# TensorE's six steady steps as one loop, in a decode-attention and gated-MLP kernel

## The chip, the cores and the metric

The kernel runs on one core of a Trainium2 chip. The metric is the device time of one execution in microseconds (us). Before the change the median of three runs is 380.52 us (380.44 to 380.76).

## The reference, cut to what matters

One token x (1024 wide) goes through two branches, and a sigmoid gate g mixes them.

```python
q = (x @ wq)                      # 32 heads of 128, in 4 groups of 8 that share one K/V head
scores = q . k_cache * 128**-0.5  # k_cache, v_cache: 4 K/V heads x 65536 positions x 128, bf16
a = softmax(scores) . v_cache @ wo
z = gelu(x @ w_in); z1, z2 = halves(z); z2 = layernorm(z2)
b = (z1 * (w_sp * z2 + b_sp)) @ w_out
g = sigmoid(sum(x * gate_w))
out = g * a + (1 - g) * b         # 1 x 1024
```

Each of the two caches is 67 MB. Together with the weights the kernel reads 162 MB and computes little on each byte.

## The kernel before, in words

**Loads.** The large loads leave SyncE (SP) on one DMA queue in a fixed order, the list `stream`: wq, K pieces, w_in, w_out, then in turn a pair of K pieces and a pair of V pieces (8 MB each), and at the end wo in five loads. They land in a ring of five slots (`RING`). `issue()` (L378) records the next load as soon as every piece that owned its place has been read; `done(key)` marks a piece as read. `halves` (L336) says which half of a pair lies first. `few_rows` (L398) carries a part of the last rows of wq in eight small loads of 4 x 5 and 4 x 3 rows of 1 KB.

**Pieces.** A K/V head is cut in four pieces of 16384 positions. A K piece is worked off in four quarters (`k_piece`, L542): VectorE (DVE) turns one quarter into one of two buffers `kt` (L548), and TensorE (PE) makes eight matmuls with it into the PSUM tensor `scp` (recorded in the helper `mm`, L261 and L263). After two pieces `score_pair` (L565) copies the scores to SBUF and takes their maximum. ScalarE (ACT) makes the exponentials and their sums `lp` (`exp_pair`, L580), DVE turns them (`pt_pair`, L585), and PE multiplies with a V piece into `ob` (`pv_piece`, L590, 32 matmuls).

**Steps.** The loop at L799 runs six steady steps, each with two K pieces, two V pieces and one `exp_pair`. In every second step a head group is closed: the maximum of the next group (`max_first`, `max_second`, with one f32 matmul at L574 that spreads it), the sums (`out_first`, two f32 matmuls at L609), the reciprocal (`out_second`), the scaling of `ob` (`out_third`), four matmuls that turn the result into columns (L627 for groups 0 and 1, L631 for groups 2 and 3), and `out_fourth`, which writes `ovz`. Groups 0 and 1 share one half-wide form, groups 2 and 3 have another. After the six steps come the last four V pieces, wo in pieces, one DVE copy (L827) and the store.

**Order.** `Recorder` notes every operation with what it reads and writes. `plan` (L57) works out the semaphore waits that are needed, and `emit` (L96) writes each engine's program straight out, operation by operation. All engines run in the order of recording; PE's program has 2313 machine instructions.

Of the kernel before, what the change touches and what calls it, by code (L numbers as in the profile page):

```python
# [13 lines left out]
class Op:  # L14
    __slots__ = ("eng", "fn", "deps", "inc", "idx", "count", "dma", "vis")


class Recorder:
# [4 lines left out]
    def __init__(self):  # L23
        self.ops = []
        self.writer = {}
        self.readers = {}
        self.dma_count = {}
        self.ahead = 0
        self.early = 0

    def op(self, eng, fn, r=(), w=(), dma=None):
        o = Op()
        o.eng, o.fn, o.inc, o.count = eng, fn, False, 0
        o.dma = None
        deps = {}
        for k in r:
            if k in self.writer:
                deps[id(self.writer[k])] = (self.writer[k], True)
        for k in w:
            if k in self.writer:  # L40
                deps.setdefault(id(self.writer[k]), (self.writer[k], False))
            for x in self.readers.get(k, ()):
                deps.setdefault(id(x), (x, False))
        o.deps = list(deps.values())
        for k in r:
            self.readers.setdefault(k, []).append(o)
        for k in w:
            self.writer[k] = o
            self.readers[k] = []
        if dma is not None:  # L50
            self.dma_count[dma] = self.dma_count.get(dma, 0) + 16
            o.dma = (dma, self.dma_count[dma])
        o.idx = len(self.ops)
        self.ops.append(o)
        return o

    def plan(self):  # L57
        known = {e: {} for e in self.ENGINES}
        waits = []
        for o in self.ops:  # L60
            kn = known[o.eng]
            need = {}
            for d, raw in o.deps:
                if d.dma is None and d.eng == o.eng and (not raw or o.eng == "PE"):
                    continue
                key = ("dma", d.dma[0]) if d.dma else d.eng
                at = d.dma[1] if d.dma else d.idx
                if kn.get(key, -1) >= at:
                    continue
                if key not in need or need[key][0] < at:  # L70
                    need[key] = (at, d)
            for key, (at, d) in list(need.items()):
                for k2, (at2, d2) in need.items():
                    if k2 != key and d2.vis.get(key, -1) >= at:
                        need.pop(key)
                        break
            mine = []
            for key, (at, d) in need.items():
                d.inc = True
                mine.append(d)  # L80
                kn[key] = max(kn.get(key, -1), at)
                for k2, a2 in d.vis.items():
                    if kn.get(k2, -1) < a2:
                        kn[k2] = a2
            waits.append(mine)
            o.vis = dict(kn)
            if o.dma is None:
                o.vis[o.eng] = o.idx
        counts = {e: 0 for e in self.ENGINES}
        for o in self.ops:  # L90
            if o.inc and o.dma is None:
                counts[o.eng] += 1
                o.count = counts[o.eng]
        return waits

    def emit(self, nc):  # L96
# [5 lines left out]
        def run(eng, handle):  # L102
            for o, ws in zip(self.ops, waits):
                if o.eng != eng:
                    continue
                for d in ws:
                    if d.dma:
                        handle.wait_ge(dsem[d.dma[0]], d.dma[1])
                    else:
                        handle.wait_ge(sems[d.eng], d.count)  # L110
# [3 lines left out]
                elif o.inc:  # L114
                    last.then_inc(sems[eng], 1)
# [12 lines left out]
        run("PE", nc.tensor)  # L128
# [7 lines left out]
        run("DVE", nc.vector)  # L136


def bass_gated_mix__gqa_block_cached__mixer_gmlp__decode_kernel(
# [53 lines left out]
    for name, n in [  # L193
# [3 lines left out]
        ("XT", KC), ("WB", 2), ("WBB", 4), ("ONEB", 128),  # L197
        ("MAXC", 2 * total), ("LP", 2 * total), ("COLS", 2 * 64), ("DM", 64), ("ONES", 256), ("QALL", 128), ("OVZ", 32 * OC + 31), ("E4Z", 128), ("MHALF", 4),
# [17 lines left out]
    idb, bm, ones = ab("IDB", 128), af("BM", 128), af("ONES", 128)  # L216
    sel, m16, mq = ab("SEL", 512), af("M16", 16), af("MQ", 16)
    xT, wb, wbb, oneb = ab("XT", KC), ab("WB", 2), af("WBB", 2), ab("ONEB", 128)
    qpad, qall = ab("QPAD", 4 * QP), ab("QALL", 128)
    maxc, lp, colt = af("MAXC", total), af("LP", total), af("COLS", 64)  # L220
# [3 lines left out]
    dm = af("DM", 32)  # L224
    psb, psb2 = ab("PSB", 1024), ab("PSB", 2048)
    osc, ot = ab("PSB", 512), af("PSB", 128, 256)
# [51 lines left out]
    P("POOL", lambda e: e.memset(ones, 1.0), w=["ones"])  # L278
# [31 lines left out]
    def load(keys, src, off):  # L310

        n = len(stream)
        w = src.shape[1]
# [22 lines left out]
    def halves(kind, n):  # L336

        a, b = (kind, n), (kind, n + 1)
        return [b, a] if n % 4 == 2 and n > 2 else [a, b]
# [20 lines left out]
    load([("wo", 0, 0)], rows(A_wo, 0, 16), WO_AT[0])  # L360
# [17 lines left out]
    def issue():  # L378

        while issued[0] < len(stream):  # L380
            n = issued[0]
            keys, off, src = stream[n]
            w = src.shape[1]
# [8 lines left out]
            P("SP", lambda e, o=OFF["RING"] + off, w=w, src=src[:, :w]: e.dma_start(arena[:, o:o + w], src),  # L392
# [82 lines left out]
    P("PE", lambda e: e.matmul(mb[:, 0:2], oneb[0:1, :], wb[0:1, :], start=True, stop=True),  # L475
# [6 lines left out]
    P("PE", lambda e: e.matmul(tb[:, 0:1], ones[0:8, :], col(C_GS)[0:8, :], start=True, stop=True),  # L482
# [59 lines left out]
    def k_piece(n, p):  # L542
        if n % NP == 0 and p == 0:
# [4 lines left out]
        P("DVE", lambda e: e.transpose(ktb(i).bitcast(F32), sl[:, 4096 * p:4096 * (p + 1)].bitcast(F32)),  # L548
          r=keys[4 * p:4 * p + 4], w=[("kt", i % NKT)])
# [12 lines left out]
        P("PE", f, r=["qpad", ("kt", i % NKT)], w=[KSC(n)])  # L562

    def score_pair(j):
        P("DVE", lambda e: e.tensor_scalar(scs(j), scp[:, :], 0.0, None, op0=ALU.add, op1=ALU.max,  # L565
                                           accum_out=maxc[:, j:j + 1]),
          w=[("sc", j % 2), ("mx", j), KSC(0), KSC(1)])

    def max_first(g):
# [4 lines left out]
        P("PE", lambda e: e.matmul(mb[:, 0:32], bm, dm, start=True, stop=True), r=["bm", "dm"], w=["mb"])  # L574

    def max_second(g):
        P("DVE", lambda e: e.tensor_reduce(gcol(g, K_NB), mb[:, 0:32], AXX, ALU.min), w=[("nb", g), "mb"])  # L577

    def exp_pair(j):
        P("ACT", lambda e: e.activation(psb2, scs(j), ACTF.Exp, bias=gcol(j // 2, K_NB), scale=SCALE,  # L580
                                        accum_out=lp[:, j:j + 1]),
          r=[("sc", j % 2), ("nb", j // 2)], w=["psb", ("lp", j)])

    def pt_pair(j):
        P("DVE", lambda e: e.transpose(ptsb2, psb2), r=["psb"], w=[("ptsb", 0), ("ptsb", 1)])  # L585
# [4 lines left out]
    def pv_piece(n):  # L590
        u = n % NP
        sl, keys = use(("v", n))

        def f(e):
            for i in range(16):
                b, t, cg = i // 8, 2 * (i % 8), i % 2
                for h in range(2):
                    ins = mm(e, h > 0, ob[64 * cg:64 * (cg + 1), 512 * h:512 * (h + 1)],
                                   ptsb(n)[:, 512 * b + 32 * t:512 * b + 32 * t + 64],
                                   vw(sl, 128 * (16 * b + t + h), [[4096, 4], [1, 128]]), start=(u == 0 and i < 2),  # L600
                                   stop=(u == NP - 1 and i >= 14), tile_position=(0, 64 * cg), skip_group_check=True)
            return ins
        P("PE", f, r=[("ptsb", n % 2)] + keys, w=["ob"])
        done(("v", n))

    def out_first(g):
        def f(e):
            for h in range(2):
                ins = e.matmul(mb[:, 0:1], bm, lp[:, 2 * g + h:2 * g + h + 1], start=(h == 0), stop=(h == 1))  # L609
            return ins  # L610
        P("PE", f, r=["bm", ("lp", 2 * g), ("lp", 2 * g + 1)], w=["mb"])

    def out_second(g):
        P("DVE", lambda e: e.reciprocal(gcol(g, K_RL), mb[:, 0:1]), w=[("rl", g), "mb"])  # L614
# [3 lines left out]
    def out_third(g):  # L618
        P("DVE", lambda e: e.tensor_scalar(osc, ob[:, 0:512], gcol(g, K_FA), None, op0=ALU.mult),
          r=[("fh", g)], w=["psb", "ob"])  # L620
        P("DVE", lambda e: e.scalar_tensor_tensor(osc, ob[:, 512:1024], gcol(g, K_FB), osc, op0=ALU.mult, op1=ALU.add),  # L621
          r=[("fh", g), "psb"], w=["psb", "ob"])

        def f(e):
            for c in range(4):
                if g < 2:
                    ins = e.matmul(mb[64 * g:64 * (g + 1), 0:128], vw(sel, 128 * c, [[2, 64]]),  # L627
                                   osc[:, 128 * c:128 * (c + 1)], start=(c == 0), stop=(c == 3),
                                   tile_position=(0, 64 * g), skip_group_check=True)
                else:  # L630
                    ins = e.matmul(mb[:, 0:128], sel[:, 128 * c:128 * (c + 1)], osc[:, 128 * c:128 * (c + 1)],  # L631
                                   start=(c == 0), stop=(c == 3))
            return ins
        P("PE", f, r=["sel", "psb"], w=["mb"])

    def out_fourth(g):

        p0, n, a, m = (64 * g, 64, 8, bm) if g < 2 else (0, 128, 16, mq)
        b, z = 128 // a, 31 + (0 if g < 2 else 256 * g)
        P("DVE", lambda e: e.tensor_tensor(vw(ot, 0, [[b, a], [1, b]], p0, n), vw(mb, 0, [[b, a], [1, b]], p0, n),  # L640
                                           vw(m, 0, [[1, a], [0, b]], p0, n), ALU.mult), r=["mq", "bm"], w=["psb", "mb"])

        def red(e):
            with nc.allow_low_precision(reason="one term is not zero"):
                return e.tensor_reduce(vw(ovz, z, [[32, b]], p0, n), vw(ot, 0, [[1, b], [b, a]], p0, n), AXX, ALU.add)
        P("DVE", red, r=["psb"], w=[("ovec", g)])

# [130 lines left out]
    def gmax(g):  # L778
        max_first(g)
        max_second(g)  # L780

    def out_rest(g):
        out_second(g)
        out_third(g)
        out_fourth(g)

# [9 lines left out]
    gmax(0)  # L796
    exp_pair(0)
    pt_pair(0)
    for i in range(6):  # L799
        k_step(2 * i + 4)  # L800
        k_step(2 * i + 5)
        score_pair(i + 2)
        pv_piece(2 * i)
        if i % 2:
            gmax((i + 1) // 2)
        exp_pair(i + 1)
        pv_piece(2 * i + 1)
        if i % 2:
            out_first(i // 2)
        pt_pair(i + 1)  # L810
        if i % 2:
            out_rest(i // 2)
# [5 lines left out]
    out_first(3)  # L818
    wo_rows()
    out_rest(3)  # L820
# [40 lines left out]
```

## Time and profile before

| what | value |
|---|---|
| median of three runs | 380.52 us |
| profiled execution | 380.59 us |
| its span, from first to last instruction | 379.3 us |
| mean granted TensorE clock | 0.838 |
| busy: PE, DVE, ACT | 229.9, 205.6, 23.3 us |
| HBM read | 162.01 MB, 427 GB/s over the span |

The span is what the views divide up; about 1.3 us of the execution lie outside it. "Busy" is the time in which an engine has at least one instruction running; the chain of waits follows the work that ended last back to what released it. The DMA table has one row for each queue and kind: packets, megabytes, and the share of the time of 16 DMA engines that their packets took.

### The profile page before, as it was taken

The page shows a single profiled execution, that of the slowest core. Times are in us where ns is not written, and L with a number is a line of the kernel's source. Part 1 is how long each engine was busy: PE and PEld are TensorE (multiplying, and loading weights), DVE is VectorE, ACT ScalarE, POOL GpSimd, SP SyncE. Part 2 cuts the span into 40 slices and gives each one's busy share as a digit, 9 for nine tenths or more (in the row PEclk, how much of TensorE's full clock was granted, in tenths as well). Part 3 has the DMA queues.
Part 4 walks back from the last instruction along what each step waited for, and adds up shares of the span by engine and source line. Part 5 has one row for each costly group of instructions (what it writes and reads, how often), then busy time and mean ns, then how long its engine had stood idle before and what let it go on. Part 6 is the DMA issues. An engine that isn't in the chain of part 4 may idle for free.

```text
span 379.3 us, 2599 instructions
## 1 busy us (share of the span) xinstructions
PE 229.9 (61%) x1452; PEld 57.9 (15%) x844; DVE 205.6 (54%) x168; ACT 23.3 (6%) x24; POOL 9.3 (2%) x36
## 2 busy tenths in 40 slices
PE   0062289566648934895389328951995189737296
PEld 0011011011201200121012001220111011201024
DVE  1411487778479625965496249745873387412020
ACT  1000000010420000002200000022000000220000
POOL 1400000000000000000000000000000000000000
PEclk9997589798959985998599959995899589958599
DMA  9999999999999999999999999999999999999896
GB/s 436 435 415 408 433 419 422 442 456 438 408 435 442 435 444 422 422 442 435 442 437 442 429 422 429 444 442 435 429 408 430 442 435 442 437 442 435 384 432 273
DMA packets 3822, 162.17 MB, mean 428 GB/s; under 512 B 484, under 2 KB 612, under 8 KB 868
## 3 DMA queue, kind: packets, MB, share of 16 engines
q1 hardware_dynamic: 3776, 162.01, 98.9%
q8 instruction: 9, 0.15, 0.1%
q10 hardware_dynamic: 36, 0.00, 0.0%
q14 instruction: 1, 0.01, 0.0%
HBM read 162.01 MB, written 0.00 MB: 427 GB/s over the span
## 4 chain that ended last, share of the span: by engine, by line
DMA 61%; PE 17%; DVE 17%; SPq 2%; ACT 1%; issue 1%
DMA arena<-in_A_k_cache_dram 46%; DVE arena L548 16%; DMA arena<-in_A_wo_dram 8%; DMA arena<-in_A_v_cache_dram 7%; PE scp L261 7%; PE scp L263 6%; SPq L409 2%; PE obt L261 2%; PE obt L263 1%; DVE arena L585 1%; PE fbt L766 1%; ACT arena L580 1%; DVE arena L670 0%; DVE arena L668 0%; PE fbt L714 0%
## 5 line engine op out<-in xcount | busy, mean ns | idle before, releaser
L548 DVE STREAM_TRANSPOSE arena<-arena 128x2048 f32<-128x2048 f32 x64 | 143.0, 2284 | 54.9 <-DMA arena<-in_A_k_cache_dram 40.1
L261 PE MATMUL scp<-arena 128*128 128x512 bf16 (+1 forms) x274 | 111.6, 424 | 94.4 <-DVE arena L548 93.9
L263 PE MATMUL scp<-arena 128*128 128x512 bf16 (+1 forms) x275 | 110.2, 418 | 0.0
L261 PE MATMUL obt<-arena 128*64 128x512 bf16 (+2 forms) x334 | 60.7, 404 | 15.1 <-DMA arena<-in_A_v_cache_dram 14.9
L263 PE MATMUL obt<-arena 128*64 128x512 bf16 (+2 forms) x333 | 60.1, 400 | 0.0
L261 PEld LDWEIGHTS scp<-arena 128*128 128x128 bf16 (+1 forms) x274 | 27.5, 104 | 205.1 <-issue 103.9
L585 DVE STREAM_TRANSPOSE arena<-arena 128x2048 bf16<-128x2048 bf16 x7 | 16.2, 2311 | 27.0 <-PE obt L263 24.8
L580 ACT ACTIVATE arena<-arena 128x2048 bf16<-128x2048 f32 x8 | 16.0, 2002 | 217.2 <-DVE arena L577 194.1
L261 PEld LDWEIGHTS obt<-arena 128*64 128x64 bf16 (+1 forms) x334 | 17.7, 109 | 65.3 <-issue 58.5
L565 DVE TENSOR_SCALAR_CACHE_REDUCE arena<-scp 128x2048 f32<-128x2048 f32 x8 | 18.3, 2292 | 16.0 <-PE scp L263 16.0
L614 DVE RECIPROCAL arena<-mbt 128x1 f32<-128x1 f32 x4 | 0.6, 138 | 17.5 <-PE mbt L609 17.5
L588 DVE STREAM_TRANSPOSE arena<-arena 128x1024 bf16<-128x1024 bf16 x2 | 2.5, 1245 | 12.9 <-PE obt L263 12.9
L536 POOL COPY arena<-arena 32x32 bf16<-32x32 bf16 x16 | 3.3, 204 | 227.4 <-PE scp L263 207.7
L467 PE MATMUL scp<-arena 8*128 8x1 bf16 x8 | 0.7, 198 | 13.0 <-DVE arena L462 13.0
L627 PE MATMUL mbt<-arena 128*64 128x128 bf16 x8 | 1.3, 314 | 7.7 <-DVE arena L621 7.7
L766 PE MATMUL fbt<-arena 128*32 128x128 bf16 x128 | 4.2, 220 | 1.2 <-DMA arena<-in_A_wo_dram 1.2
L280 DVE MEMSET mbt<- 128x512 f32 x1 | 0.5, 485 | 7.7 <-PEq L846 7.7
L513 DVE CAST arena<-obt 97x1024 bf16<-97x1024 f32 x1 | 1.2, 1224 | 6.2 <-PE obt L507 6.2
L475 PE MATMUL mbt<-arena 1*128 1x2 bf16 x1 | 0.2, 158 | 7.2 <-DMA arena<-in_B_b_sp_dram 7.2
L827 DVE CAST arena<-fbt 36x128 bf16<-36x128 f32 x1 | 0.3, 283 | 7.3 <-PE fbt L766 7.3
L477 DVE COPY arena<-mbt 128x2 f32<-128x2 f32 x1 | 0.2, 158 | 7.3 <-PE mbt L475 7.3
L577 DVE TENSOR_REDUCE arena<-mbt 128x1 f32<-128x32 f32 x4 | 0.8, 192 | 6.0 <-PE mbt L574 6.0
(99 smaller groups left out, 62.5 us busy)
## 6 DMA issues: line engine op xcount, KB each, us to landing
arena<-in_A_k_cache_dram SPq DMA_DIRECT2D x2, 4096.0 KB, 31.7
arena<-in_A_wq_dram SPq DMA_DIRECT2D x1, 8064.0 KB, 21.7
arena<-in_B_w_in_dram SPq DMA_DIRECT2D x1, 7168.0 KB, 28.9
arena<-in_A_wo_dram SPq DMA_DIRECT2D x1, 4096.0 KB, 38.5
arena<-in_B_w_out_dram SPq DMA_DIRECT2D x1, 3584.0 KB, 20.2
arena<-in_A_wo_dram SPq DMA_DIRECT2D x1, 2048.0 KB, 27.6
arena<-in_A_wo_dram SPq DMA_DIRECT2D x1, 1280.0 KB, 30.3
arena<-in_A_wo_dram SPq DMA_DIRECT2D x1, 512.0 KB, 31.0
```

The source lines that it names most:

```text
L261: return e.matmul(*a, **kw)
L263: one = e.matmul(*a, **kw).ins
L409: P("SP", lambda e, a=a, b=b: e.dma_start(a, b), w=[("few", lo + j0)] + ([] if lo + j0 else [("slot", x) for x in gr]), dma="few%d" % (lo ...
L513: P("DVE", lambda e: e.tensor_copy(psb[0:97, :], ob[0:97, :]), w=["psb", "ob"])
L536: P("POOL", lambda e, pb=pb: e.tensor_copy(vw(qpad, 24 + 32 * pb, [[QP, 4], [1, 8]], 32 * pb, 32), vw(qall, 8 * g, [[32, 4], [1, 8]], 32 * ...
L548: P("DVE", lambda e: e.transpose(ktb(i).bitcast(F32), sl[:, 4096 * p:4096 * (p + 1)].bitcast(F32)), r=keys[4 * p:4 * p + 4], w=[("kt", i % ...
L565: P("DVE", lambda e: e.tensor_scalar(scs(j), scp[:, :], 0.0, None, op0=ALU.add, op1=ALU.max, accum_out=maxc[:, j:j + 1]), w=[("sc", j % 2) ...
L580: P("ACT", lambda e: e.activation(psb2, scs(j), ACTF.Exp, bias=gcol(j // 2, K_NB), scale=SCALE, accum_out=lp[:, j:j + 1]), r=[("sc", j % 2 ...
L585: P("DVE", lambda e: e.transpose(ptsb2, psb2), r=["psb"], w=[("ptsb", 0), ("ptsb", 1)])
L588: P("DVE", lambda e: e.transpose(ptsb(n), ab("PSB", 1024, 1024 * (n % 2))), r=["psb"], w=[("ptsb", n % 2)])
L627: ins = e.matmul(mb[64 * g:64 * (g + 1), 0:128], vw(sel, 128 * c, [[2, 64]]), osc[:, 128 * c:128 * (c + 1)], start=(c == 0), stop=(c == 3) ...
L766: ins = e.matmul(fb[32 * b:32 * (b + 1), 0:QW], ovz[:, z:z + 32], sl[:, o:o + QW], start=False, stop=(i == 3 and c == 7), tile_position=(0 ...
```

## The change

- PE's part of the six steps is emitted once and runs in a hardware loop of six turns. A wait in the loop reads its threshold from a register, which a register addition then raises. For this every turn must have the same instructions and equal steps of every counter: `even()` adds to some of DVE's increments. The waits inside are only those named by `on=`.
- Every step now has the spread matmul (one, of 34 columns instead of 32: maximum and sums together) and the four turning matmuls, also the steps that close no group. `out_first` and its two f32 matmuls go.
- DVE gets `sums` (a copy of 128x2 into `dm`), a `tensor_reduce` of 128x2 in `out_second`, and `clear` (a memset of `ob`, 128x1024) ahead of the loop and after each closed group. Matmuls into `ob` always add.
- All four head groups leave in the form that groups 2 and 3 had. wo's first load has rows in two blocks of 8 x 128 (256 packets of 16 KB instead of 128 of 32 KB). V pairs keep one order of halves. `osc` gets a place of its own.
- The wait for q's layout (`qpad`) moves from PE to the K transposition on DVE.

The diff, cut to its core:

```diff
+    def even(self):
+        body = [o for o in self.ops if o.loop]
+        told = {o.loop[1] for o in body if o.inc}
+        for o in body:
+            o.inc = o.loop[1] in told
...
                 for d in ws:
-                    if d.dma:
-                        handle.wait_ge(dsem[d.dma[0]], d.dma[1])
+                    sem, n = (dsem[d.dma[0]], d.dma[1]) if d.dma else (sems[d.eng], d.count)
+                    if o.loop:
+                        reg, step = count[d.dma[0] if d.dma else d.eng, o.loop[1]]
+                        handle.wait_ge(sem, reg)
+                        handle.reg_add(reg, reg, step)
                     else:
-                        handle.wait_ge(sems[d.eng], d.count)
+                        handle.wait_ge(sem, n)
...
+        lead = next(o.idx for o in self.ops if o.loop)
+        run("PE", nc.tensor, lambda o: not o.loop and o.idx < lead)
+        for reg, n in begin:
+            nc.tensor.reg_mov(reg, n)
+        with nc.Fori(0, turns, engines=[mybir.EngineType.PE]):
+            run("PE", nc.tensor, lambda o: o.loop and o.loop[0] == 0)
+        run("PE", nc.tensor, lambda o: not o.loop and o.idx > lead)
...
-    load([("wo", 0, 0)], rows(A_wo, 0, 16), WO_AT[0])
+    load([("wo", 0, 0)], A_wo[0:2048, :].rearrange("(g p c) n -> p g (c n)", g=2, p=128), WO_AT[0])
...
+    def sums():
+        return P("DVE", lambda e: e.tensor_copy(dm[:, 32:34], lp), r=[("lp", 0), ("lp", 1)], w=["dm"], mark="g")
+    def spread_columns(on=None):
+        P("PE", lambda e: e.matmul(mb[:, 0:34], bm, dm, start=True, stop=True), r=["bm", "dm"], w=["mb"], on=on and [on])
+    def clear():
+        P("DVE", lambda e: e.memset(ob, 0.0), w=["ob"])
...
     for i in range(6):
+        R.begin(i)
         k_step(2 * i + 4)
         k_step(2 * i + 5)
-        score_pair(i + 2)
+        known = score_pair(i + 2)
+        if i % 2:
+            max_first((i + 1) // 2)
+            known = sums()
         pv_piece(2 * i)
+        spread_columns(known)
         if i % 2:
-            gmax((i + 1) // 2)
+            max_second((i + 1) // 2)
+            out_second(i // 2)
         exp_pair(i + 1)
         pv_piece(2 * i + 1)
+        known = pt_pair(i + 1)
         if i % 2:
-            out_first(i // 2)
-        pt_pair(i + 1)
+            known = out_third(i // 2)
+        turn_heads(known)
         if i % 2:
-            out_rest(i // 2)
+            out_fourth(i // 2)
+            clear()
```

## The prediction, as put on record

> **What bounds the kernel now.** I read the page first: slices and DMA table, then the chain.
>
> ```profile
> DMA  9999999999999999999999999999999999999896
> ...
> q1 hardware_dynamic: 3776, 162.01, 98.9%
> q8 instruction: 9, 0.15, 0.1%
> ...
> DMA 61%; PE 17%; DVE 17%; SPq 2%; ACT 1%; issue 1%
> ```
>
> The data queue keeps the 16 DMA engines busy for 98.9% of the span, in every slice but the last. So the stream of 162 MB is the bound. PE (61% busy) and DVE (54%) stand in the chain only because a load is issued when they have freed its place. The chain in order of time shows the end:
>
> ```profile
> 345.07 30.26 DMA arena<-in_A_wo_dram
> 375.46 1.80 PE fbt L766 x56
> 377.27 0.42 PE fbt L766 x8
> 377.72 0.28 DVE arena L827
> ```
>
> The last load lands at 377.23, and 2.1 us of matmuls, copy and store follow. The time can change in three ways: the stream starves, the DMA engine that ends last gets more or less to do, or the tail changes.
>
> **How much cover there is.** The timeline of the first two steady steps:
>
> ```profile
> 135.93 0.33 SPq L392 DMA_DIRECT2D arena<-in_A_v_cache_dram  x1
> 136.02 2.31 DVE L585 STREAM_TRANSPOSE arena<-arena 128x2048 bf16<-128x2048 bf16 x1 [4.82 <-PE obt L263]
> 145.33 2.31 DVE L548 STREAM_TRANSPOSE arena<-arena 128x2048 f32<-128x2048 f32 x1 [7.00 <-DMA arena<-in_A_k_cache_dram]
> ```
>
> A step without a closing group ends its DVE work at 138.33 and idles 7.0 us until the next K pair lands. The next step closes a group and idles 3.92 us:
>
> ```profile
> 176.63 0.13 DVE L614 RECIPROCAL arena<-mbt 128x1 f32<-128x1 f32 x1
> ...
> 180.03 2.00 ACT L580 ACTIVATE arena<-arena 128x2048 bf16<-128x2048 f32 x1 [6.97 <-DVE arena L645]
> ...
> 183.92 2.31 DVE L548 STREAM_TRANSPOSE arena<-arena 128x2048 f32<-128x2048 f32 x1 [3.92 <-DMA arena<-in_A_k_cache_dram]
> ```
>
> The second cover is the issue. I set each issue of SP beside the first completion of the load ahead of it. The V issue at 135.93 is followed by a K landing at 143.32: 7.4 us ahead. In the loop the K issues are 5.8 us (118.15 against 123.98) to 7.2 us ahead, the V issues 7.4 to 8.3. The very first issue, at 0.00, had its first packet at 1.18. So the shortest cover is 5.83 - 1.18 = 4.6 us.
>
> **The change part by part.**
>
> *DVE.* `clear` writes 128x1024 f32 in PSUM: twice the 128x512 memset (485 ns), 0.97 us. `sums` is near the 128x2 copy of L477, 0.16 us. The 128x2 reduce lies between a 128x1 operation, 0.16, and the 128x32 reduce, 0.19. The wider `out_fourth` costs nothing: 0.29 + 0.39 us at 128 partitions against 0.28 + 0.36. Together about 1.3 us in each closing step. The reciprocal and scaling (0.4) move ahead of `pt_pair`, so about 0.9 us of it lies before the next K landing, where 3.92 us are idle: nothing on the path. The first `clear` must wait until ACT has copied `ob` (100.93); it delays the first maximum from 102.05 to about 102.3, and the K issue at 118.15 by as much, out of 4.6.
>
> *PE.* A plain step gains one f32 spread (0.41 us, L574) and four turning matmuls (0.40 to 0.63, L631 and L627): 1.0 us. A closing step loses the two f32 matmuls of L609 (0.61). In a plain step the turning matmuls wait for `pt_pair`, which ended at 138.33. Behind them in PE's queue stand the K matmuls, which can't start before 145.33 + 2.3: 9 us of cover. In a closing step they stand where they stood. The spread waits for `score_pair` (131.20 in the first step), which is done before the V piece ahead of it (about 132): no wait. V's issue comes 0.4 us later, out of at least 6.2.
>
> *Loop control.* No row shows a register wait, a register addition or a branch. Their bound from below is nothing, because PE waits for data between them. From above I take the 0.9 us of idle PE (192.34 against 191.43) right behind one instruction fetch, for each of the eleven waits: 10 us a step. But only the first two or three quarters of a K pair wait for PE (L548 at 151.33 behind 1.5 us); then DVE at 2.2 us a quarter sets the pace. So at most 2 to 3 us reach a K issue, under 4.6. I take nothing, nearest to the rows of L261 that follow their release within 0.1 us.
>
> *wo's first load.* 256 packets of 16 KB for 128 of 32 KB: a 16384-byte packet took 611 ns, a 32768-byte one 1213. Eight packets more per engine at 2 x 611 - 1213 = 9 ns: +0.07 us on the stream.
>
> *Instruction packets.* This is what the loop can change in the stream. PE's queue fetched nine packets of 16384 bytes, at 48.8, 94.7, 133.4, 191.4, 242.3, 285.6, 329.0, 370.9 and 377.2; 147456 bytes for 2311 records is 64 bytes each, 256 instructions a packet. Five steps of 204 to 216 instructions go, so about four packets. As bytes this is 65 KB at 428 GB/s, 0.15 us. But each packet sits on one DMA engine, and what counts is the engine that ends last. Each load reports 16 completions, one per engine. At 42.09 eleven engines end within 0.4 us of the first and five are 1.10 to 1.58 behind (the 1 KB rows of `few_rows` went to five engines). After each PE packet the leading group has one member fewer, set back some 1.2 us: ten at 57, nine at 107, four at 338. The last engine is one of the five: 1.1 behind, then about 0.9 more after a single 8 KB instruction packet at 85.05, 1.9 to 2.05 behind from there to the end. No PE packet hit it. So fewer PE packets leave the leaders ahead and the last engine where it is. **The gain is nothing**, between -0.6 (an even stream: the mean lag at the end is about 1.25 against 1.88) and nothing.
>
> *Sum.* 380.59 (the profiled execution, 0.07 above the median) + 0.07 + nothing: against the median 380.6.
>
> **Rivals.**
>
> *The body is fetched again in every turn (slower).* Place: the backward branch. Eight packet distances are 2048 instructions; 2295 had started at the ninth packet, so the sequencer reached its first boundary at 247 or more while 185 had started: it reads some 62 ahead. The third boundary is then at 759 to 775. The loop's body starts at 543 plus a few register moves and holds some 217: its end is at 763 to 766. So the boundary falls either behind the loop or into its last instructions. In the second case every turn crosses it, fetches the block behind, and has to get the first block back. That is two to three packets a turn: 2 ahead of the loop, 11 to 16 in it, 2 or 3 behind, 15 to 21. It decides from the point where more packets come than there are leading engines, 11: then the five late ones are hit, 1.2 us each. The last to land is then one at 1.5 + 1.2 (against 1.88, +0.8) up to one at 1.9 + 1.3 (+1.3): 381.4 to 381.9. For it: the boundary is that near. Against it: most of the interval lies behind the loop.
>
> The Trainium skill ("Runtime: NRT & Kernel Launch", Instruction fetch mechanics) says the same mechanism: a taken branch whose target isn't in the present two-page window forces a fetch of the target page before execution goes on. The same section gives TensorE room for 2048 instructions, by which nothing would be fetched again. The trace agrees with pages of 256 and fetching in sequence; without a branch it can't show which holds.
>
> *The same fetch stalls PE beyond its cover (slower).* A closing step has PE free at 179.3 and the next K matmul at 186.3; a fetch above 7 us would delay K's issue, and above 7 + 4.6 starve the stream. The longest packet took 1.06 us. Price: the excess, three times.
>
> *A second 8 KB packet (slower).* The one at 85.05 came when 59 DVE records had started; 8192 bytes are 128 more, 187. DVE has 177 records, after the change 177 + 12 = 189, so a second may come in the tail. It costs nothing on a leading engine, 0.5 to 0.95 on a late one: up to 381.5.
>
> *The last engine is relieved (faster).* If fewer fetches shift the 8 KB packet to another engine, the end comes 0.15 to 0.6 earlier: 380.0 to 380.4. Against: that packet comes before the loop.
>
> *The loop doesn't save fetches but adds none beyond the leaders*: same time, 380.6.
>
> **How the numbers follow.** A measurement of this kernel tells 0.2%, 0.76 us, from no change. The forecast with its equal-time variants has 0.58, the refetch 0.28, the second packet on a late engine 0.05, the stall 0.03, the relief 0.06. Faster by over 0.2% needs the whole relief: 0.05. Slower: 0.28 + 0.05 + 0.03 = 0.36. Same: 0.59. Predicted 380.6. The range goes from 380.2 (part of the relief) to 381.8, most of the refetch; the likeliest case's own range is 380.4 to 380.9.
>
> **What would show it.** Right: four to five packets in PE's instruction queue, DMA share of 98.9% unchanged, the issue of every load still 5 us or more ahead, the last landing at 377.2 to 377.4. Refetch: 15 or more instruction packets, and the leading group of engines gone before the last loads. Wrong altogether: slices with DMA under 9 in the loop (starving), or a tail that no longer is 2.1 us.

## The result and the profile after

The changed kernel takes 381.06 us (median of 22 runs, 380.91 to 381.32) against 380.45 us (22 runs, 380.29 to 380.76): a ratio of 1.0017, 95% interval 1.0010 to 1.0023. It is slower by 0.61 us, within the 0.2% that I had called "the same", but with an interval that lies clear of 1. The profiled execution has a span of 380.0 us against 379.3; at 381.32 us it is the slowest of the 22, so the traces differ by a little more (0.73 us) than the medians.

From the page of the changed kernel, the busy share of the DMA engines, the DMA queues (packets, MB, share of 16 engines) and the chain:

```profile
DMA  9999999999999999999999999999999999999895
...
q1 hardware_dynamic: 3904, 162.01, 98.8%
q8 instruction: 5, 0.08, 0.1%
q14 instruction: 2, 0.02, 0.0%
...
DMA 66%; PE 17%; DVE 12%; SPq 2%; issue 1%; ACT 1%; DVEq 0%
```

The stream is as full as before. PE's instruction packets (q8) went from nine to five. The row to look at is q14: two packets where there was one. The 128 packets more in q1 are wo's first load. Before the change the row of q14 read:

```profile
q14 instruction: 1, 0.01, 0.0%
```

The end of the chain in order of time (start, length, what):

```profile
344.28 31.85 DMA arena<-in_A_wo_dram
376.13 0.14 issue
376.26 2.15 PE fbt L839 x64
378.42 0.02 issue
378.44 0.28 DVE arena L907
```

By the DMA records the last load lands at 377.95 against 377.23, 0.72 us later; from there to the end of the span it is 2.05 us against 2.03 (spans of 380.00 and 379.26 us). So all of the time came in the stream, and none in the tail.

The 16 completions of the last load, one per DMA engine, show where in the stream. Lag behind the first engine to finish, in us, sorted:

```
before (first at 375.34): 0 .08 .25 .96 1.34 1.36 1.38 1.44 1.45 1.46 1.47 1.50 1.53 1.60 1.67 1.89
after  (first at 375.26): 0 .07 .12 .13 .31 .38 .58 .75 1.29 1.33 1.34 1.37 1.51 1.56 1.57 2.69
```

Eight engines instead of three are now less than 0.8 behind. Four of these five are packets that PE no longer fetches while data flows; the fifth was less far behind from the start (twelve engines under 0.9 at 42 us, against eleven). The first engine ends 0.08 earlier. But one engine ends 2.69 behind, and a load has landed when its last engine is done. In the load that lands at 338 the last engine is 1.89 behind; in the next, at 358, it is 2.82. Between them, at 347.60, stands q14's second packet, 8192 bytes. Here is DVE at that time, from the timeline (start, length):

```profile
347.36 1.25 DVE L670 STREAM_TRANSPOSE arena<-arena 128x1024 bf16<-128x1024 bf16 x1 [2.14 <-PE obt L326]
348.53 0.13 DVE L652 COPY arena<-arena 128x2 f32<-128x2 f32 x1
368.12 0.16 DVE L691 TENSOR_REDUCE arena<-mbt 128x1 f32<-128x2 f32 x1 [19.47 <-PE mbt L655]
```

The transposition at 347.36 is DVE's 190th record. The first 8 KB packet came at 83.84, when 59 had started: 131 records apart, against the 128 instructions that 8192 bytes hold.

The covered parts stayed covered. DVE in the first plain and the first closing step:

```profile
136.26 2.31 DVE L666 STREAM_TRANSPOSE arena<-arena 128x2048 bf16<-128x2048 bf16 x1 [5.21 <-PE obt L326]
145.25 2.31 DVE L619 STREAM_TRANSPOSE arena<-arena 128x2048 f32<-128x2048 f32 x1 [6.67 <-DMA arena<-in_A_k_cache_dram]
...
179.39 0.91 DVE L688 MEMSET obt<- 128x1024 f32 x1 [0.21 <-issue]
...
183.78 2.31 DVE L619 STREAM_TRANSPOSE arena<-arena 128x2048 f32<-128x2048 f32 x1 [3.48 <-DMA arena<-in_A_k_cache_dram]
```

Before the next K pair lands, DVE still idles 6.67 us (7.00 before) and 3.48 us (3.92 before). In the loop SP's issues are 6.0 to 7.9 us ahead of the stream, 5.8 to 8.3 before. The rival of a starving stream is out.

### The profile page after: what moved, and what is told of

Same layout as the page of the kernel before. It is cut to its first block, busy times and chain, and to the rows that moved or that the text cites. A ratio compares the mean times of both kernels' runs of the same rounds, so it can differ in the third digit from the quotient of the medians.

```text
span 380.0 us, 2709 instructions
## 1 busy us (share of the span) xinstructions
PE 232.5 (61%) x1456; PEld 58.1 (15%) x848; DVE 209.6 (55%) x180; ACT 23.2 (6%) x24; POOL 9.5 (3%) x38
## 4 chain that ended last, share of the span: by engine, by line
DMA 66%; PE 17%; DVE 12%; SPq 2%; issue 1%; ACT 1%; DVEq 0%
DMA arena<-in_A_k_cache_dram 46%; DVE arena L619 11%; DMA arena<-in_A_wo_dram 8%; DMA arena<-in_A_v_cache_dram 7%; PE scp L324 6%; PE scp L326 6%; DMA arena<-in_A_wq_dram 4%; PE obt L324 2%; PE obt L326 2%; SPq L480 1%; PE fbt L839 1%; ACT arena L661 1%; PE obt L578 0%; SPq L463 0%; ACT arena L783 0%
## 5 line engine op out<-in xcount | busy, mean ns | idle before, releaser
L324 PE MATMUL obt<-arena 128*64 128x512 bf16 (+2 forms) x334 | 61.4, 412 | 16.0 <-DMA arena<-in_A_v_cache_dram 15.8
L326 PE MATMUL obt<-arena 128*64 128x512 bf16 (+2 forms) x333 | 60.8, 408 | 0.0
L706 PE MATMUL mbt<-arena 128*128 128x128 bf16 x28 | 3.1, 242 | 19.9 <-DVE arena L699 12.1
L706 PEld LDWEIGHTS mbt<-arena 128*128 128x128 bf16 x28 | 1.9, 105 | 24.6 <-issue 23.7
L688 DVE MEMSET obt<- 128x1024 f32 x4 | 3.6, 912 | 1.5 <-ACT arena L783 0.8
```

The source lines that it names most:

```text
L324: return e.matmul(*a, **kw)
L326: one = e.matmul(*a, **kw).ins
L688: P("DVE", lambda e: e.memset(ob, 0.0), w=["ob"])
L706: ins = e.matmul(mb[:, 128:256], sel[:, 128 * c:128 * (c + 1)], osc[:, 128 * c:128 * (c + 1)], start=(c == 0), stop=(c == 3))
```

## The experiments

**Theory:** the time is set by the DMA engine that ends last; DVE's second 8 KB packet falls on that engine and sets it back by 0.9 us; all else in the change nets to about nothing. **Rivals:** the loop (register waits, branch) costs the time; DVE's additional work costs it; the branch fetches again.

**The packet without the change.** The kernel before, with 24 memsets of 128x1 on DVE, at places where it idles:

```diff
         if i % 2:
             out_rest(i // 2)
+        for k in range(4):
+            P("DVE", lambda e, o=2 * (4 * i + k): e.memset(ab("SPARE", 2, o), 0.0))
```

> The kernel before, with four 128x1 memsets on DVE at the end of each of the six steps (24 in all, a spare place, nothing reads it). Packet theory: DVE passes its second block boundary at about 330 us, a second 8 KB instruction packet appears in the DMA records, on the engine that is already last; the spread of the last load's 16 completions goes from 1.89 to about 2.8 and the time from 380.45 to 381.0 to 381.2, with no loop and no other part of the change in it. Rival (the loop, or wo's 256 packets, costs the 0.6 us): no change, 380.45.

Measured: 381.08 us against 380.45 (ratio 1.0016, 1.0007 to 1.0026). Queues, and the memsets after the last step:

```profile
q8 instruction: 9, 0.15, 0.1%
q14 instruction: 2, 0.02, 0.0%
```

```profile
333.76 0.08 DVE L814 MEMSET arena<- 128x1 uint32 x4
```

The second packet came at 332.85. The last engine's lag went from 1.61 at 319 us to 2.44 at 339. At the end of the stream it is 2.28, less than the 2.8 expected, because the row stood at 1.6 and not at 1.89 ahead of the packet; the rise of 0.67 is near the 0.63 us of the time. The row shows four memsets in 0.08 us together, so the 24 are 0.5 us of work, in steps that idle 3.9 us or more, and they alone give the whole 0.63 us.

**The same, below the boundary.** One memset a step, six in all (the same edit with one in place of four):

> The same with one memset a step, six in all: DVE's records go from 177 to 183, below the boundary that the changed kernel passed with 190. Packet theory: no second 8 KB packet, spread 1.9, time 380.45 as before. Rival (more DVE instructions cost time by their work or their waits): a quarter of what the 24 cost.

Measured: 380.73, ratio 1.0007 (0.9998 to 1.0016). No second packet, spread 1.76, span 379.1 as before. But 0.28 us were there all the same, and they lie outside the span: 1.67 us (median) against 1.35. Two runs follow that up.

**Two memsets, and twelve:**

> The kernel before with two 128x1 memsets on DVE in all (one at the end of each of the first two steps), 179 records. The six memsets of an earlier run cost 0.28 us with no second packet and an unchanged span of 379.1: the time lay outside the span (1.67 against 1.35). Theory: DVE's program end reaches the second block boundary just after the span, and the packet is fetched there; with only two more the end stays ahead of the boundary: 380.45, 1.35 outside the span. Rival (each DVE instruction costs some 0.05 us): 380.55. Rival (a constant of each program, whatever it holds): any value.

> The same with twelve memsets, two a step, 189 records. Theory: the boundary is reached in the last microseconds, while DVE waits for the last copy or before; a second 8 KB packet either shows behind 368 us, too late to set the last engine back by its full 0.9 us, or falls behind the span: 380.5 to 381.1. Rival (each DVE instruction costs some 0.05 us): 381.0 with no second packet. Rival (a constant of each program): any value.

Measured: 380.50 with two, 380.57 with twelve, both against 380.56 (ratios 0.9997 and 1.0000, both +-0.0009). With twelve the second packet is there:

```profile
q8 instruction: 9, 0.15, 0.1%
q14 instruction: 2, 0.02, 0.0%
```

It comes at 379.22, behind the last data packet, and costs nothing that shows within the 0.3 us of the interval; 0.05 us for each instruction would have been 0.6. So neither DVE's work nor the packet as such costs the 0.6 us; a packet costs when it falls into the stream. The 0.28 us of the six memsets don't follow the number of instructions, and no trace shows a packet for them; the last section comes back to them.

**The loop undone.** The changed kernel with PE's steps written out, and two memsets in each plain step, so that DVE has as many instructions as in the loop version:

```diff
-        R.begin(i)
...
-        with nc.Fori(0, turns, engines=[mybir.EngineType.PE]):
-            run("PE", nc.tensor, lambda o: o.loop and o.loop[0] == 0)
...
+        run("PE", nc.tensor)
...
+        else:
+            for k in range(2):
+                P("DVE", lambda e, o=2 * (2 * i + k): e.memset(ab("SPARE", 2, o), 0.0))
```

> The changed kernel with TensorE's six steps written out again, and two 128x1 memsets on DVE in each plain step so that DVE has about as many instructions as in the loop version. Packet theory: nine 16 KB packets of PE again, the second 8 KB packet of DVE stays, and the time stays at 381.0 to 381.2. Rival (the loop's register waits and its branch cost the 0.6 us): 380.4 to 380.5.

Measured: 381.17 (ratio 1.0019, 1.0009 to 1.0028), nine PE packets, the second DVE packet at 349.73, and the last engine's lag from 1.75 to 2.42. Without the loop the loss stays: the loop doesn't cause it, and its four packets fewer gain nothing that shows.

**The packet taken away.** The changed kernel, loop and all, with 13 instructions fewer on DVE; the main edits:

```diff
-        return P("DVE", lambda e: e.tensor_copy(dm[:, 32:34], lp), ...
+        return P("DVE", lambda e: e.tensor_reduce(dm[:, 32:33], lp, AXX, ALU.add), ...
...
-        P("DVE", lambda e: e.tensor_reduce(gcol(g, K_L), mb[:, 32:34], AXX, ALU.add), ...
-        P("DVE", lambda e: e.reciprocal(gcol(g, K_RL), gcol(g, K_L)), ...
+        P("DVE", lambda e: e.reciprocal(gcol(g, K_RL), mb[:, 32:33]), ...
...
-        if n < 14:
-            pt_half(n + 2)
+        if n == 13:
+            pt_pair(7)
```

> The changed kernel, loop and all, with 13 fewer DVE instructions: two memsets gone, the two sums added before the spread matmul, one transposition for the last pair, six small operations at the start on ScalarE and GpSimd. Packet theory: no second 8 KB packet before 377 us, spread 1.9, time 380.4 to 380.6. Rival (the loop, wo's packets or the other new work cost it): 381.0 to 381.1 still. Both: something between.

Measured: 380.63 (ratio 1.0003, 0.9994 to 1.0012). From its page:

```profile
q8 instruction: 5, 0.08, 0.1%
...
q14 instruction: 1, 0.01, 0.0%
```

With one q14 packet the lag at the end is 1.62 and the median span 379.1, as in the kernel before. The median is 0.18 above it, inside the interval; 0.08 of this lies outside the span. So most of the 0.61 us is gone, and the rest can't be told from nothing. The edit also lightens DVE elsewhere, but twelve operations more on DVE had cost nothing that shows, with no packet in the stream.

**Does the branch fetch again?** The changed kernel with 60 small matmuls ahead of the first K piece, so that the loop's body starts 120 instructions later:

```diff
+    def f(e):
+        for k in range(60):
+            ins = e.matmul(tb[:, 0:32], idb, idb[:, 0:32], start=True, stop=True)
+        return ins
+    P("PE", f, r=["idb"], w=[KTB])
```

> The changed kernel with 60 small matmuls (128x32, about 120 more PE instructions) on PE ahead of the first K piece, where PE waits for data. The loop's 217 instructions then begin 120 later and lie across a block boundary of 256 instead of just ahead of one. Theory that both blocks stay with PE: one packet more than the five at the most, spread and time as in the changed kernel, 381.0 to 381.1. Rival (each backward branch fetches again): 15 or more PE packets, the leading engines gone, the last engine hit as well, 381.5 to 382.5; a stall of PE of 1 to 4 us at the head of each turn that stays behind its cover.

Measured: 381.18 (ratio 1.0018, 1.0009 to 1.0027), and:

```profile
q8 instruction: 5, 0.08, 0.1%
q14 instruction: 2, 0.02, 0.0%
```

Five packets still. One came in the first turn, at 130.7, with 808 PE records started, and none in the five turns after it; the next is at 346, behind the loop. Wherever in my interval of 759 to 775 the boundary lies, the body, from 665 to 882, lies across it. The rows of the five taken branches last 0.21 to 0.23 us in its trace, the same as in the changed kernel, so no stall shows there. The refetch rival is refuted for a body of this size, which lies in two blocks of 256; a body over three blocks was not run.

**A faster version?** The lean kernel with wq loaded evenly, without the small loads that burden five engines (the core of the edit; the operations that served the small loads go too):

```diff
-            cut = keys == [("wq", 0)]
+            cut = False
```

> The lean version of the loop kernel (no second 8 KB packet) with wq loaded whole and evenly, without the eight small loads of 1 KB rows that burden five engines. Theory (the engine that ends last sets the time): all engines get 8 KB more, 0.3 us; the five late ones get 0.74 to 1.47 us less; the last is then an engine that one 16 KB packet hit, 1.2 to 1.4 behind, so the last landing comes 0.2 to 0.4 earlier than in the kernel before: 380.1 to 380.4. Rival (the small loads don't matter for the end): 380.6 or, with 0.3 us more on every engine, 380.9.

Measured: 380.88 (ratio 1.0014, 1.0005 to 1.0023): a miss. Half of the mechanism came as expected: in the load that lands at 41 us the first engine ends at 40.71, 0.37 later than in the lean version, and no engine is more than 0.37 behind it (1.98 there). But the four engines that a PE packet has hit end 1.43 to 1.62 behind, not 1.2 to 1.4. With the first engine at 375.67 the last landing is at 377.29, and nothing is gained. The median span is 0.2 us longer than in the kernel before, and 0.23 us more lie outside it, as with the six memsets. No version beat the kernel before.

## Why the prediction was right or wrong

The time lies in the predicted range (380.2 to 381.8) and in the likeliest band (within 0.2%), but above the likeliest case's own range (380.4 to 380.9). The forecast of 380.6 is 0.46 low. That the range holds the time is luck in part: its upper half was there for the refetch, which did not come, and the packet that cost the time had a chance of 0.05.

- *The bound, the cover, the tail:* right. The stream is full in every slice but the end, no issue came late, the tail is the same 2.1 us.
- *DVE work:* right in kind. `clear` was estimated at 0.97 us and took 0.912 (a row of the kernel before, L281, had the same shape at 912 ns); `sums` at 0.16 and took 0.13 to 0.16. The idle time left before the K landing shrank by 0.3 and 0.4 us and costs nothing.
- *Loop control and PE's new matmuls:* nothing that shows, as taken. The unrolled version is no faster, and the lean version has both and loses at most little.
- *wo's first load:* expected +0.07; the first engine ended it 9.72 us after the load ahead of it, against 9.67.
- *Instruction packets of PE:* right. Five came, engines that lead were left ahead, and the last engine stayed the last: no gain. One size was off: a PE packet was taken to set its engine back by some 1.2 us. Before the change the leaders lie within 0.3, and one engine stands at 1.72 after the packet at 94.73 and one at 1.81 after that at 242.34, so it is 1.4 or more. In the prediction only the price of the refetch rested on it. The mean lag at the end is 1.21, not 1.25.
- *The refetch,* 0.28 of the chance: wrong. The Trainium skill ("Runtime: NRT & Kernel Launch", Instruction fetch mechanics) says that a taken branch out of a two-page window forces a fetch. The straddling loop, whose body lies in two blocks, shows none in five backward branches. The room for 2048 instructions on TensorE that the same section of the Trainium skill gives agrees with that run.
- *The second 8 KB packet:* this is the step that failed. The prediction described it with its place, its boundary and its price ("0.5 to 0.95 on a late one", "up to 381.5"), and gave it 0.05. Two terms of it were wrong. The count: "177 + 12 = 189" took operations for instructions. The trace of after has 199 DVE records. The ten more are semaphore events that stand alone: 18 against 8. Four of them stand ahead of the K transpositions that now wait for the layout of q and a DMA at once. Six stand in the plain steps, beside the operations whose increments `even()` raised above one. And the engine: I took it as a matter of chance which one is hit. In every run with two packets inside the stream (the changed kernel, the 24 memsets, the unrolled and the straddling version) the second hit an engine of the late group and made it the last. In two of them the rows let one follow it: in the changed kernel it was the last engine (1.89 to 2.82), in the straddling version the one next to last (1.54 to 2.51), and each had been put at that place by the first packet. In the other two the late engines lie too close together to tell which was hit.

With 199 the packet comes at 347.6, and everything behind it follows: 0.93 us on that engine, 0.72 at the landing in the trace, 0.61 in the median.

## What to carry to other kernels

Where DMA bounds a kernel, compare the completions of one load engine by engine: here the last engine set the time, and a change that relieved the others showed nothing. Count an engine's program in instructions, not operations, waits and raised increments included, and see which fetch boundary the new count passes and whether data still flows then. Twelve added instructions cost nothing where 24 cost 0.63 us.

## What the hardware showed that I had not expected

- An instruction packet costs its DMA engine more than its own time: 8192 bytes took 309 ns and set the engine back by 0.93 to 0.97 us where the rows let one follow it (before, the changed kernel, the straddling version); 16384 bytes took 0.88 to 1.06 us while data flowed and set it back by 1.4 us or more. Why stays open.
- PE's packets in the kernel before fell each on another engine that led; DVE's two packets fell on one and the same, in the two runs whose lags can show it.
- Two programs took 0.2 to 0.3 us more outside the span than the kernel before. Sorted by their DVE records, the medians outside the span are 1.35 us with 177, 1.30 with 179, 1.56 with 182 (the even wq), 1.67 with 183 (six memsets), 1.43 with 186 (lean), 1.37 with 189, and 1.32 to 1.35 with 199 and 201. So the addition comes only where DVE's program ends just below the boundary. This fits the theory on record for the two memsets, a packet fetched right behind the span. No trace reaches that far, so it is argued and not shown.
